# Moving the first mixture's low parts to VectorE, with two weight factors in flight and another queue order

## The chip, the cores and the metric

The kernel runs on one core of a Trainium2 chip. The metric is the device time of one launch in microseconds (us). Before the change it is 1488.94 us, the median of three runs (1488.45 to 1491.52). The core has five instruction queues that run side by side: TensorE (PE, with its weight loads as PEld), VectorE (DVE), ScalarE (ACT), GpSimd (POOL) and SyncE (SP), which here only issues DMAs. Each queue runs its own instructions in the order in which they stand in it, and waits on semaphores for the others.

## The reference, cut to what matters

Three layers follow one another: clustered attention, a feed-forward layer ("first mixture"), and a gated mixture of eight experts ("second mixture"). The change lies in the first mixture, which is

```python
h = x @ w_in                      # (1536, 512) @ (512, 2048)
g = h * (1.0 / (1.0 + np.exp(-h)))
return (g @ w_out).astype(np.float32)   # (1536, 2048) @ (2048, 512)
```

## The kernel before

All matrix products are made in fp32 accuracy from faster fp32r multiplications: each factor is rounded to a high part (a copy on ScalarE into an fp32r tile), the low part is the difference `lo = x - hi`, and a product is the sum of high x high, high x low and low x high. So each factor costs one rounding copy and one subtraction.

The first mixture is worked in four slices of 512 of the 2048 inner columns (`s` = 0 to 3). A slice has 19 steps (`u`). In steps 0 to 6 `h` is made by seven block products of a Strassen-Winograd scheme (`aproduct`, 24 matmuls each, numbers 1, 5, 6, 3, 7, 2, 4 in this order). In steps 7 to 18 twelve output tiles `y0` to `y11` are made (`ytile`, 12 or 16 matmuls each) and added into the accumulator (`total`, on ScalarE in slice 0, on VectorE after it). Product 4 of the seven (fourth counted from 0, number 7) adds into PSUM banks that product 6 uses again, so product 6 must wait for VectorE's additions `aevac`, which read these banks.

Around the products stand these pieces, named by the lines of the kernel before:

- `w_steps` (lines 82 to 100) *narrows* a quarter (128 x 512 values) of a float64 weight, read as two 32-bit words, to fp32: `wb` and `w0` on ScalarE (L88, L89), `w1` to `w4` on VectorE (L90 to L93), `wp0`, the product with the scale, on GpSimd (L94), `wp1`, an addition on VectorE (L95). A slice of `w_out` (odd `n`) is also split at once into `woh` (`wh`, ScalarE, L98) and `wol` (`wp2`, GpSimd, L99).
- `mfactor` (L120 to L125) makes the weight factor of a block product: `vh` on ScalarE (L123), `vl` on GpSimd (L124). Three pairs of buffers rotate.
- `gsilu`, `ghi`, `glo` (L665 to L679) take a finished block of `h` through silu, rounding (`gh`) and subtraction (`gl`, on GpSimd, L679).
- `split` and `five` (L127, L383) make the token-side factors from `xa`, `xb`, `xc`, which attention leaves behind; `xlo` (L367) writes them.
- `put(s, u, ...)` (L741 to L791) says at which step of which slice each of these pieces is issued; within a step the order is that of the `put` lines, after the additions and totals of the step. That order is the order in each queue. In attention a table of words (`ORDER`) does the same.

After the four slices the second mixture begins. Its first factors (`factor`, `x_factor`, `w_sums1`, L871 to L946) are written to the queues by a scheduler among the last twelve output tiles; their tiles lie in memory that the first mixture leaves.

Of the kernel before, what the change touches and what calls it, by code (L numbers as in the profile page):

```python
# [38 lines left out]
def attention_moe_kernel(ctx, tc, kq, vp, cent, w_in, w_out, w_gate, w1, w2, out):  # L39
# [687 lines left out]
    def narrow(n, k, keys):  # L727
        if (n, k) not in quarters:
            if n % 2:
                a = rp.tile([P, 1, FB], F32, name=f"a{n}_{k}", tag="na", bufs=1)  # L730
# [4 lines left out]
        for key in keys.split():
            quarters[n, k][key]()
            if key == "wp0":
                m = 4 * (n - 1) + k + 2
                load(1 + m // 4, m % 4)

    for s in range(NS1):  # L741
        n = 2 * s + 1
# [10 lines left out]
        put(s, 1, narrow, n, 1, "w1 w2")
        put(s, 2, mfactor, s, 4)
        put(s, 2, narrow, n, 0, "wp1 wh wp2")
        put(s, 2, narrow, n, 1, "w3 w4 wp0")
        put(s, 2, narrow, n, 2, "wb w0")
        put(s, 2, narrow, n, 2, "w1")
        if s == 0:
            put(s, 1, split, 7, xb)  # L760
            put(s, 2, split, 4, xa)
        put(s, 3, mfactor, s, 5)
        put(s, 3, narrow, n, 1, "wp1 wh wp2")
        put(s, 3, narrow, n, 2, "w2 w3 w4 wp0")
        put(s, 4, mfactor, s, 6)
# [560 lines left out]
```

## Time and profile before

| quantity | value |
|---|---|
| median of three runs | 1488.94 us |
| profiled execution | 1492.27 us |
| span inside it, first to last instruction | 1490.3 us |
| PE busy in the span | 1449.8 us (97%) |
| DVE, ACT, POOL busy | 1086.8, 948.6, 483.6 us |
| first mixture: first product to last output tile | 240.4 to 521.9 us |
| granted TensorE clock, mean over the span | 0.99 |

A row of a timeline gives the start, the duration, the engine, the line of the kernel, the operation with its tiles, and in brackets how long the engine had been idle before it and what ended that. A tile is named without its numbers there: `vl`, `gl` and `wol` are the low parts, `vh`, `gh` and `woh` the high parts, `y` an output tile, `b` and `raw` the pieces of the narrowing. In a row of a table by windows the first number is the length of the window, then each engine's busy time, and after the engines the granted TensorE clock as a share of full speed.

### The profile page before, as it was taken

Reading aid. Unit: us, or ns where it says so; the run is one execution under the profiler, and the core shown is the slowest. Engines: PE = TensorE matmul, PEld = TensorE weight load, DVE = VectorE, ACT = ScalarE, POOL = GpSimd, SP = SyncE. Lnnn points to the kernel's source line nnn. Section 1 sums busy time; section 2 is a strip of 40 time slices with the busy share of each in tenths; the row PEclk is TensorE's granted clock in tenths of the full one; section 3 lists DMA queues with packets and bytes.
Section 4 is the critical chain, followed back from the end, with each engine's and each line's share of the span. In section 5 each row is a group of like instructions: output and inputs, shape, how many; then the busy total and the mean of one; then the engine's idle time right before and its main releaser. Section 6 shows DMA issues by size and latency. Waiting matters only on the chain.

```text
span 1490.3 us, 25085 instructions
## 1 busy us (share of the span) xinstructions
PE 1449.8 (97%) x9785; PEld 1296.6 (87%) x9785; DVE 1086.8 (73%) x1658; ACT 948.6 (64%) x1782; POOL 483.6 (32%) x432
## 2 busy tenths in 40 slices
PE   8999998898989899999999999999999999999998
PEld 5777776787878779999999999999999999999998
DVE  7788877757777498958668577686685776866858
ACT  6677665655445257567576576675765766757655
POOL 6677744747565301020222221211211201112111
PEclk9999999899999999999999999999999999999999
DMA  7665511121212005393797987956958759569586
GB/s 205 188 167 152 139 49 45 56 71 57 71 58 100 0 29 134 74 203 81 168 159 132 189 133 141 195 86 120 159 92 160 125 96 191 90 116 166 89 149 128
DMA packets 136311, 177.48 MB, mean 119 GB/s; under 512 B 6272, under 2 KB 108672, under 8 KB 136192
## 3 DMA queue, kind: packets, MB, share of 16 engines
q0 software_dynamic: 83584, 87.30, 38.7%
q1 hardware_dynamic: 51104, 87.32, 19.4%
q8 instruction: 77, 1.26, 0.3%
q10 hardware_dynamic: 1504, 1.25, 0.3%
q14 instruction: 42, 0.34, 0.1%
HBM read 65.36 MB, written 88.87 MB: 103 GB/s over the span
## 4 chain that ended last, share of the span: by engine, by line
PE 83%; DVE 9%; ACT 3%; issue 2%; POOL 2%; DMA 0%; DVEq 0%; ACTq 0%; POOLq 0%
PE b L637 31%; PE a L637 29%; PE y L691 9%; PE av L341 4%; PE t L319 3%; PE s L282 2%; PE s L284 2%; PE l L637 2%; DVE a L92 1%; DVE h L663 1%; DVE m L291 1%; POOL wol L99 1%; DVE h L844 1%; POOL gl L679 1%; DVE b L95 1%
## 5 line engine op out<-in xcount | busy, mean ns | idle before, releaser
L637 PE MATMUL b<-wfh,ah 128*128 128x256 f32 x1344 | 381.3, 284 | 1.2 <-ACT ah L1059 1.2
L637 PE MATMUL b<-wfh,al 128*128 128x256 f32 x1344 | 381.0, 283 | 0.7 <-DVE al L1069 0.7
L637 PE MATMUL b<-wfl,ah 128*128 128x256 f32 x1344 | 380.8, 283 | 0.0
L1131 POOL DMA_DIRECT2D out_dram<-acc x87 | 126.3, 1607 | 572.5 <-ACT acc L1122 388.0
L637 PE MATMUL a<-xfh,wfh 128*128 128x512 f32 (+1 forms) x896 | 302.5, 338 | 0.0
L637 PE MATMUL a<-xfl,wfh 128*128 128x512 f32 (+1 forms) x896 | 302.0, 337 | 0.0
L637 PE MATMUL a<-xfh,wfl 128*128 128x512 f32 (+1 forms) x896 | 301.3, 336 | 0.0
L637 PEld LDWEIGHTS b<-wfh,ah 128*128 128x128 f32 x1344 | 258.1, 192 | 1.5 <-ACT ah L1059 1.4
L637 PEld LDWEIGHTS b<-wfh,al 128*128 128x128 f32 x1344 | 258.1, 192 | 1.1 <-DVE al L1069 1.1
L637 PEld LDWEIGHTS b<-wfl,ah 128*128 128x128 f32 x1344 | 258.1, 192 | 0.0
L1122 ACT ACTIVATE acc<-b,Pg 128x256 f32<-128x256 f32 x484 | 186.3, 475 | 21.8 <-issue 20.4
L847 DVE TENSOR_TENSOR al<-h,ah 128x768 fp32r<-128x768 f32 x192 | 177.7, 955 | 30.0 <-ACT ah L1061 29.4
L1061 ACT CAST ah<-h 128x768 fp32r<-128x768 f32 x192 | 160.6, 841 | 50.1 <-PE b L637 24.0
L637 PEld LDWEIGHTS a<-xfh,wfh 128*128 128x128 f32 x896 | 170.1, 190 | 19.6 <-issue 0.6
L637 PEld LDWEIGHTS a<-xfh,wfl 128*128 128x128 f32 x896 | 169.9, 190 | 18.0
L637 PEld LDWEIGHTS a<-xfl,wfh 128*128 128x128 f32 x896 | 170.1, 190 | 17.5
L847 DVE TENSOR_TENSOR wfl<-w0r,wfh 128x512 fp32r<-128x512 f32 x96 | 66.5, 708 | 81.1 <-ACT wfh L932 78.9
L844 DVE TENSOR_TENSOR h<-a,h 128x512 f32<-128x512 f32 x144 | 94.3, 686 | 26.5 <-PE a L637 25.7
L300 ACT ACTIVATE p<-s,m 128x768 f32<-128x768 f32 x96 | 86.6, 903 | 42.1 <-DVE m L291 39.4
L1048 ACT COPY h<-a 128x512 f32<-128x512 f32 x144 | 81.1, 590 | 48.2 <-PE a L637 48.1
L310 POOL TENSOR_SCALAR p<-p,rec 128x768 f32<-128x768 f32 x96 | 85.6, 904 | 55.0 <-DVE rec L305 45.0
L291 DVE TENSOR_REDUCE m<-s 128x1 f32<-128x768 f32 x96 | 89.9, 951 | 17.0 <-PE s L284 16.6
(221 smaller groups left out, 2690.8 us busy)
## 6 DMA issues: line engine op xcount, KB each, us to landing
out_dram<-acc POOLq DMA_DIRECT2D x91, 768.0 KB, 9.5
w0r<-in_w_dram SPq DMA_DIRECT2D x16, 1024.0 KB, 7.5
w1r<-in_w_dram SPq DMA_DIRECT2D x16, 1024.0 KB, 6.7
qk<-qk SPq DMA_DIRECT2D x45, 192.0 KB, 3.6
raw<-in_w_out_dram SPq DMA_DIRECT2D x16, 512.0 KB, 3.4
first_out<-acc POOLq DMA_DIRECT2D x10, 768.0 KB, 10.1
raw<-in_kq_dram SPq DMA_DIRECT2D x16, 384.0 KB, 4.2
raw<-in_w_in_dram SPq DMA_DIRECT2D x12, 512.0 KB, 3.7
```

The lines of the kernel that those rows point to most:

```text
L291: nc.vector.tensor_reduce(out=m, in_=tiles[i]["s"][:, :S], axis=AX.X, op=ALU.max, negate=True)
L300: nc.scalar.activation(t["p"], t.pop("s")[:, :S], AF.Exp, bias=t.pop("m"), accum_out=chunks[c]["sum"][:, j, 0:1])
L310: nc.gpsimd.tensor_scalar(out=p, in0=p, scalar1=chunks[c]["rec"][:, j : j + 1], scalar2=1.0, op0=ALU.mult, op1=ALU.mult)
L341: nc.tensor.matmul(ps[o * D : (o + 1) * D, :CW], lhsT=vr[2 * pair + o][:, kt, :], rhs=pts[o][:, kt, :], start=kt == 0, stop=kt == NT - 1, ...
L637: nc.tensor.matmul(ps[u][:, cols], lhsT=lf(i, k), rhs=rt(j, k), start=fresh and u not in opened, stop=k == 1 and q == 2, skip_group_check= ...
L691: nc.tensor.matmul(out, lhsT=w[:, k, d * P : (d + 1) * P], rhs=g, start=first, stop=last, skip_group_check=True)
L844: e.tensor_tensor(out=out, in0=in0, in1=in1, op=op)
L847: e.tensor_tensor(out=lo, in0=x, in1=r(hi), op=ALU.subtract)
L1048: act.copy(bank(t, u), ps[u])
L1061: act.copy(hi, x)
L1122: act.mul(t[:, 2 * u + m], z[:, m], g)
L1131: gps.dma_start(out=to, in_=t, accum_op=ALU.add)
```

## The change

All subtractions of the first mixture (`vl`, `wol`, `gl`) go from GpSimd to VectorE; GpSimd keeps only the narrowing's products `wp0`. Two pairs of factor buffers rotate instead of three, and the factors of products 2 to 6 are issued at the head of steps 1 to 5, ahead of that step's copies out of PSUM. Two `a` and three `b` buffers of the narrowing stand instead of one and two. The `put` lines are rearranged: the quarters of `w_out` are narrowed earlier, the first quarter of a later slice already in steps 17 and 18 of the slice before it. The last difference of the tokens goes into a tile of its own (`xd`), the factors of product 5 are made later in attention, and the sums `sums1` too. In the second mixture the pool of the weight sums (`wsp`) lies ahead of the token factors in memory.

```diff
-            got["wp2"] = lambda: nc.gpsimd.tensor_tensor(out=lo, in0=b, in1=r(hi), op=ALU.subtract)
+            got["wp2"] = lambda: nc.vector.tensor_tensor(out=lo, in0=b, in1=r(hi), op=ALU.subtract)
...
-        hi, lo = ((wf0 if n % 3 == 0 else wfpool[0]).tile([P, 2, FB // 2], F32R, name=f"v{c}{n}", tag=f"v{c}") for c in "hl")
+        hi, lo = ((wf0 if n % 2 == 0 else wfpool[0]).tile([P, 2, FB // 2], F32R, name=f"v{c}{n}", tag=f"v{c}") for c in "hl")
         nc.scalar.copy(hi, x)
-        nc.gpsimd.tensor_tensor(out=lo, in0=x, in1=r(hi), op=ALU.subtract)
+        nc.vector.tensor_tensor(out=lo, in0=x, in1=r(hi), op=ALU.subtract)
...
-            v(out=xa[at], in0=ps, in1=xc[at], op=ALU.subtract)
+            v(out=xd[at], in0=ps, in1=xc[at], op=ALU.subtract)
...
-    wfpool[0] = pool(mctx, "wfq", bufs=2)
+    wfpool[0] = pool(mctx, "wfq", bufs=1)
...
-            nc.gpsimd.tensor_tensor(out=t[:, m], in0=hblk[f, h][:, m], in1=r(gh)[:, h, 2 * f + m], op=ALU.subtract)
+            nc.vector.tensor_tensor(out=t[:, m], in0=hblk[f, h][:, m], in1=r(gh)[:, h, 2 * f + m], op=ALU.subtract)
...
         if s == 0:
             put(s, 0, mfactor, 0, 1)
+            put(s, 0, narrow, n, 0, "wb w0")
             put(s, 0, split, 6, xc)
-        put(s, 0, mfactor, s, 2)
+            put(s, 0, narrow, n, 0, "w1 w2 w3 w4 wp0")
+        put(s, 0, narrow, n, 0, "wp1 wh wp2")
         put(s, 0, sum4)
...
+        put(s, 0, narrow, n, 1, "wb w0 w1 w2 w3 w4 wp0")
         put(s, 1, sum3)
...
+        put(s, 4, narrow, n, 3, "wp1 wh wp2")
+        put(s, 4, ghi, 3)
+        if s == 0:
+            put(s, 4, split, 4, xd)
...
+            put(s, 17, narrow, n, 0, "wb w0 w1 w2")
+            put(s, 18, narrow, n, 0, "w3 w4 wp0")
...
+                if 1 <= u <= 5:
+                    mfactor(s, u + 1)
                 if 1 <= u <= 7:
                     aevac(s, u - 1)
...
     w2p = pool(ctx, "w2p", bufs=1)
+    wsp = pool(ctx, "wsp", bufs=2)
     xfp = pool(ctx, "xfp", bufs=1)
     wfp = pool(ctx, "wfp", bufs=5)
-    wsp = pool(ctx, "wsp", bufs=2)
```

VectorE's queue at the start of the first slice, before the change (`yl6`, `yl7` are token factors, `raw1_k`, `a1_k`, `b1_k` belong to quarter k of the first `w_out` slice):

```order
L381 TENSOR_TENSOR xa_81<-av23_3104,xc_83 128x256
L90 TENSOR_SCALAR raw1_0_3159<-raw1_0_3159 128x512
L91 TENSOR_SCALAR raw1_0_3159<-raw1_0_3159 128x512
L132 TENSOR_TENSOR yl6_3151<-xc_83,yh6_3150 128x768 x2
L115 TENSOR_TENSOR win_84<-win_84,wsum_85 128x2x256
L92 SCALAR_TENSOR_TENSOR a1_0_3165<-raw1_0_3159 128x512
L93 TENSOR_SCALAR raw1_0_3159<-a1_0_3165 128x512
```

The same queue from the same instruction after the change:

```order
L381 TENSOR_TENSOR xd_84<-av23_3105,xc_83 128x256
L124 TENSOR_TENSOR vl1_3167<-win_85,vh1_3166 128x512
L132 TENSOR_TENSOR yl6_3152<-xc_83,yh6_3151 128x768 x2
L90 TENSOR_SCALAR raw1_0_3160<-raw1_0_3160 128x512
L91 TENSOR_SCALAR raw1_0_3160<-raw1_0_3160 128x512
...
L95 TENSOR_TENSOR b1_0_3171<-a1_0_3170,b1_0_3171 128x512
L99 TENSOR_TENSOR wol_3159<-b1_0_3171,woh_3158 128x512
L115 TENSOR_TENSOR win_85<-win_85,wsum_86 128x2x256
L90 TENSOR_SCALAR raw1_1_3162<-raw1_1_3162 128x512
...
L124 TENSOR_TENSOR vl2_3228<-wsum_86,vh2_3227 128x512
```

The low part `vl2`, which product 2 needs, was on GpSimd before; it now stands behind the whole narrowing of quarter 0 and four steps of quarter 1.

ScalarE's queue in the last steps of the products of slice 1, after the change (line numbers of the changed kernel; L674 is silu, L679 the rounding of its result):

```order
L123 CAST vh12_3912<-win_85 128x512
L674 ACTIVATE h1_6_3877<-h1_6_3877 128x768 x2
L98 CAST woh_3158<-a3_3_3842 128x512
L679 CAST gh_3157<-h1_6_3877 128x768 x2
L123 CAST vh13_3950<-win_85 128x512
```

Before the change `vh13` stood right behind `vh12` and one `woh`, ahead of the silu. VectorE's queue there, after the change (L669 is an addition out of PSUM):

```order
L124 TENSOR_TENSOR vl12_3913<-win_85,vh12_3912 128x512
L669 TENSOR_TENSOR h1_6_3877<-l1_5_1_3803,h1_6_3877 128x512
...
L95 TENSOR_TENSOR b3_3_3843<-a3_3_3842,b3_3_3843 128x512
L99 TENSOR_TENSOR wol_3159<-b3_3_3843,woh_3158 128x512
L124 TENSOR_TENSOR vl13_3951<-win_85,vh13_3950 128x512
L669 TENSOR_TENSOR h1_5_3833<-l1_1_0_3757,h1_5_3833 128x512
...
L685 TENSOR_TENSOR gl1_3_3957<-h1_6_3877,gh_3157 128x768 x2
...
L685 TENSOR_TENSOR gl1_7_3994<-h1_5_3833,gh_3157 128x768 x2
```

The additions for product 6's banks (`h1_5`) stand behind `vl13`. Last, VectorE's queue at the end of the first mixture, before (`y3_7` to `y3_11` are left out, `wfl`, `xfl`, `w0r` and `ws` belong to the second mixture):

```order
L714 TENSOR_TENSOR acc1_3477<-y3_0_5121,acc1_3477 128x512
L847 TENSOR_TENSOR wfl0_5363<-w0r0_5358,wfh0_5362 128x512
L847 TENSOR_TENSOR wfl1_5367<-w0r0_5358,wfh1_5366 128x512
...
L847 TENSOR_TENSOR xfl1_5371<-acc1_3477,xfh1_5370 128x768
L714 TENSOR_TENSOR acc1_3477<-y3_5_5195,acc1_3477 128x2x256
L847 TENSOR_TENSOR xfl1_5371<-acc1_3477,xfh1_5370 128x768
L844 TENSOR_TENSOR w0r0_5358<-w0r0_5358 128x2x256
...
L714 TENSOR_TENSOR acc1_3477<-y3_11_5291,acc1_3477 128x512
L844 TENSOR_TENSOR ws0_5376<-w0r0_5358 128x512
```

and after, in the changed kernel's line numbers (L720 is the total, L851 and L848 are L847 and L844 of before):

```order
L720 TENSOR_TENSOR acc1_3480<-y3_11_5292,acc1_3480 128x512
L851 TENSOR_TENSOR wfl0_5364<-w0r0_5359,wfh0_5363 128x512
L851 TENSOR_TENSOR wfl1_5368<-w0r0_5359,wfh1_5367 128x512
L851 TENSOR_TENSOR xfl1_5372<-acc1_3480,xfh1_5371 128x768 x2
L848 TENSOR_TENSOR w0r0_5359<-w0r0_5359 128x2x256
L848 TENSOR_TENSOR ws0_5377<-w0r0_5359 128x512
```

Five subtractions and sums that stood among the last totals now stand behind the last one. The order of TensorE's and SyncE's queues is the same in both kernels.

## Rows read from the trace of the kernel before

**Rows 1.** Waits of PE in 230 to 525 us: total us, times, longest us

```profile
PE y L691 <- POOL wol L99: 10.8, 4, 2.7
PE y L691 <- POOL gl L679: 6.0, 4, 2.4
PE l L637 <- ACT h L659: 3.7, 1, 3.7
```

**Rows 2.** Busy time by windows: products and output tiles of the slices

```profile
240.40:269.80 29.40, 25.66 (x139) 22.22 (x139) 25.85 (x30) 21.19 (x35) 16.94 (x11) 0.94 0.21 65
269.80:283.20 13.40, 8.33 (x42) 6.49 (x41) 10.28 (x10) 10.66 (x17) 12.15 (x8) 0.95 0.17 55
...
316.80:346.00 29.20, 29.20 (x169) 25.84 (x168) 24.56 (x28) 20.67 (x34) 19.76 (x14) 1.00 0.17 55
346.00:352.50 6.50, 2.53 (x11) 1.45 (x9) 3.53 (x4) 5.50 (x9) 6.50 (x5) 0.83 0.27 81
352.50:385.60 33.10, 33.10 (x151) 27.80 (x152) 22.79 (x33) 9.04 (x15) 16.48 (x11) 0.93 0.21 64
...
421.20:453.80 32.60, 32.59 (x151) 27.38 (x152) 22.92 (x33) 9.07 (x15) 16.54 (x11) 0.95 0.21 65
...
489.50:522.00 32.50, 32.50 (x151) 27.28 (x152) 13.04 (x16) 5.33 (x8) 7.92 (x4) 0.95 0.00 1
```

**Rows 3.** PE's timeline: end of the gap before slice 1's output tiles

```profile
352.48 0.79 PE L691 MATMUL y<-gh,wol 128*128 128x512 f32 x1 [2.71 <-POOL wol L99]
```

**Rows 4.** VectorE's timeline, steps of the narrowing and additions, slices 0 and 1

```profile
299.33 0.43 DVE L91 TENSOR_SCALAR raw<-raw 128x512 uint32<-128x512 uint32 x1
299.80 0.69 DVE L92 SCALAR_TENSOR_TENSOR win<-raw 128x512 uint32<-128x512 uint32 x1
...
302.43 0.69 DVE L95 TENSOR_TENSOR win<-win,b 128x512 f32<-128x512 f32 x1 [1.48 <-POOL b L94]
...
319.48 1.78 DVE L115 TENSOR_TENSOR win<-win,wsum 128x512 f32<-128x512 f32 x1
...
336.11 1.87 DVE L663 TENSOR_TENSOR h<-l,h 128x512 f32<-128x512 f32 x3
```

**Rows 5.** The page's group of VectorE's 128x768 subtractions in the second mixture

```profile
L847 DVE TENSOR_TENSOR al<-h,ah 128x768 fp32r<-128x768 f32 x192 | 177.7, 955 | 30.0 <-ACT ah L1061 29.4
```

**Rows 6.** GpSimd's timeline: two low parts and a product of the narrowing

```profile
232.84 1.27 POOL L124 TENSOR_TENSOR vl<-win,vh 128x512 fp32r<-128x512 f32 x1 [1.46 <-PE av L341]
...
319.23 1.49 POOL L124 TENSOR_TENSOR vl<-wsum,vh 128x512 fp32r<-128x512 f32 x1 [2.67 <-ACT vh L123]
...
336.32 1.32 POOL L94 TENSOR_TENSOR b<-b,raw 128x512 f32<-128x512 f32 x1 [0.42 <-PE l L637]
```

**Rows 7.** ScalarE's timeline: narrowing, token factor, weight factor, silu, rounding

```profile
240.81 0.67 ACT L88 ACTIVATE b<-raw 128x512 f32<-128x512 uint32 x1
...
242.64 1.57 ACT L130 CAST yh<-xc 128x768 fp32r<-128x768 f32 x2
...
332.16 0.62 ACT L123 CAST vh<-win 128x512 fp32r<-128x512 f32 x1
...
337.42 1.58 ACT L668 ACTIVATE h<-h 128x768 f32<-128x768 f32 x2
...
339.41 1.57 ACT L673 CAST gh<-h 128x768 fp32r<-128x768 f32 x2
```

**Rows 8.** VectorE's timeline around the last total

```profile
508.08 0.69 DVE L844 TENSOR_TENSOR w0r<-w0r 128x512 f32<-128x512 f32 x1
...
522.11 0.69 DVE L714 TENSOR_TENSOR acc<-y,acc 128x512 f32<-128x512 f32 x1 [2.03 <-PE y L691]
```

**Rows 9.** PE's timeline, start of the second mixture and end of attention

```profile
529.20 1.71 PE L971 MATMUL gl<-acc,wgr 128*32 128x384 f32 x12 [2.21 <-DVE acc L844]
...
235.05 1.86 PE L319 MATMUL t<-ident,p 128*128 128x128 f32 x12 [0.79 <-POOL p L310]
```

**Rows 10.** Busy time by windows around that start

```profile
528.00:532.00 4.00, 2.79 (x22) 1.47 (x22) 3.97 (x6) 1.67 (x2) 0.00 (x0) 1.00 0.00 0
532.00:536.00 4.00, 4.00 (x21) 3.29 (x20) 3.44 (x4) 3.19 (x6) 0.00 (x0) 1.00 0.00 0
```

More of the change, by code (lines that the diff above doesn't have):

```diff
@@ L59, in attention_moe_kernel @@
     yf = {p: x_tiles(p, xpool) for p in (1, 3, 2)}
-    xa, xb, xc = (xap.tile([P, 2, S], F32, name=f"x{c}") for c in "abc")
+    xa, xb, xc, xd = (xap.tile([P, 2, S], F32, name=f"x{c}") for c in "abcd")
     NS1 = F1 // FB
@@ L380, in xlo, with five @@
         else:
-            v(out=xa[at], in0=ps, in1=xc[at], op=ALU.subtract)
-    def five(k):
+            v(out=xd[at], in0=ps, in1=xc[at], op=ALU.subtract)
+    def five():
         if 5 not in yf:
@@ L386, in five, with five_hi, five_lo @@
             yf[5] = (both[:, 0], both[:, 1])
-        split(5, xa, (k,))
+        return yf[5]
+    def five_hi(k):
+        nc.scalar.copy(five()[0][:, k], xa[:, k])
+    def five_lo(k):
+        nc.vector.tensor_tensor(out=five()[1][:, k], in0=xa[:, k], in1=r(five()[0][:, k]), op=ALU.subtract)
     def wd(k):
@@ L412, in attention_moe_kernel @@
         KINDS[key] = (wstep(key), 1, 0, 4)
-    KINDS["y5a"] = (lambda i: five(0), 1, 6, 7)
-    KINDS["y5b"] = (lambda i: five(1), 1, 6, 7)
+    KINDS["h5"] = (five_hi, 1, 0, 2)
+    KINDS["l5"] = (five_lo, 1, 0, 2)
     KINDS["s1"] = early(sums1)
@@ L421, in attention_moe_kernel @@
         wp0,-2 T,-1 evD,-3 S,3 evD,-1 lv,2 evA,-2 wp1,-2 sim,1,0 rec,0 lv,1 av,-1 mx,2 ld,5 nrm,0 mx,3 ex,2 nrm,1 ex,3 split,3 S,4 xh,-1 rec,1
-        wb,-1 w0,-1 xl,-1 y5a,0 T,0 sims,1 mx,4 T,1 evA,0 nrm,2 S,5 sd,3 evD,1 ex,4 simt,1,1 nrm,3 T,2 mx,5 cc,2 T,3 evA,2 split,2 T,4 cha,1 ex,5 T,5 chb,1 S,6
-        evD,4 evA,3 S,7 chc,1 evA,5 mx,6 av,0 chd,1 ex,6 mx,7 chs,1 rec,2 ex,7 sd,2 nrm,4 S,8 chr,1 rec,3 xh,0 nrm,5 oht,1,0 mx,8 T,6 mr,1 S,9
-        nrm,6 xl,0 y5b,0 s1,0 ex,8 md,1 T,7 evD,6 nrm,7 T,8 mx,9 evA,7 T,9 castm,4 evA,8 T,10 evD,9 ex,9 T,11 castm,5 evD,10 ld,6 S,10 evA,11 wd,0 w1,-1 S,11
+        wb,-1 w0,-1 xl,-1 T,0 sims,1 mx,4 T,1 evA,0 nrm,2 S,5 sd,3 evD,1 ex,4 simt,1,1 nrm,3 T,2 mx,5 cc,2 T,3 evA,2 split,2 T,4 cha,1 ex,5 T,5 chb,1 S,6
+        evD,4 evA,3 S,7 chc,1 evA,5 h5,-6 mx,6 av,0 chd,1 ex,6 mx,7 chs,1 rec,2 ex,7 sd,2 nrm,4 S,8 l5,-6 chr,1 rec,3 xh,0 nrm,5 oht,1,0 mx,8 T,6 mr,1 S,9
+        nrm,6 xl,0 ex,8 md,1 T,7 evD,6 nrm,7 T,8 mx,9 evA,7 T,9 castm,4 s1,0 evA,8 T,10 evD,9 ex,9 T,11 castm,5 evD,10 ld,6 S,10 evA,11 wd,0 w1,-1 S,11
         rec,4 w2,-1 av,1 mx,10 castd,5 nrm,8 mx,11 ex,10 nrm,9 ex,11 f0,0
@@ L729, in narrow @@
             if n % 2:
-                a = rp.tile([P, 1, FB], F32, name=f"a{n}_{k}", tag="na", bufs=1)
-                b = rp.tile([P, 1, FB], F32, name=f"b{n}_{k}", tag="nb")
+                a = rp.tile([P, 1, FB], F32, name=f"a{n}_{k}", tag="na")
+                b = rp.tile([P, 1, FB], F32, name=f"b{n}_{k}", tag="nb", bufs=3)
                 quarters[n, k] = w_steps(n, k, a, b, wo_h[:, k : k + 1], wo_l[:, k : k + 1])
             else:
-                quarters[n, k] = w_steps(n, k, win[:, :, k * P : (k + 1) * P], rp.tile([P, 4, P], F32, name=f"b{n}_{k}", tag="nb"))
+                quarters[n, k] = w_steps(n, k, win[:, :, k * P : (k + 1) * P], rp.tile([P, 4, P], F32, name=f"b{n}_{k}", tag="nb", bufs=3))
         for key in keys.split():
@@ L742, in attention_moe_kernel @@
         n = 2 * s + 1
-        put(s, 0, narrow, n, 0, "wb w0 w1 w2")
         if s == 0:
             put(s, 0, mfactor, 0, 1)
+            put(s, 0, narrow, n, 0, "wb w0")
             put(s, 0, split, 6, xc)
-        put(s, 0, mfactor, s, 2)
+            put(s, 0, narrow, n, 0, "w1 w2 w3 w4 wp0")
+        put(s, 0, narrow, n, 0, "wp1 wh wp2")
         put(s, 0, sum4)
-        put(s, 1, mfactor, s, 3)
-        put(s, 1, narrow, n, 0, "w3 w4 wp0")
-        put(s, 1, narrow, n, 1, "wb w0")
+        put(s, 0, narrow, n, 1, "wb w0 w1 w2 w3 w4 wp0")
@@ L752, in attention_moe_kernel @@
         put(s, 1, sum3)
[L753 to L758, printed above, removed]
-        if s == 0:
[L760 to L765, printed above, removed]
@@ L766, in attention_moe_kernel @@
-        put(s, 4, narrow, n, 3, "wb w0")
+        put(s, 1, narrow, n, 1, "wp1 wh wp2")
+        put(s, 1, narrow, n, 2, "wb w0 w1 w2")
+        if s == 0:
+            put(s, 2, split, 7, xb)
+        put(s, 2, narrow, n, 2, "w3 w4 wp0")
+        put(s, 2, narrow, n, 3, "wb w0")
+        put(s, 2, narrow, n, 2, "wp1 wh wp2")
+        put(s, 3, narrow, n, 3, "w1 w2 w3 w4 wp0")
         put(s, 4, gsilu, 3)
-        put(s, 4, narrow, n, 2, "wp1 wh wp2")
-        put(s, 4, narrow, n, 3, "w1")
-        put(s, 5, ghi, 3)
+        put(s, 4, narrow, n, 3, "wp1 wh wp2")
@@ L771, in attention_moe_kernel @@
+        put(s, 4, ghi, 3)
+        if s == 0:
+            put(s, 4, split, 4, xd)
         put(s, 5, glo, s, 3)
         put(s, 5, gsilu, 7)
-        put(s, 5, narrow, n, 3, "w2 w3 w4 wp0")
-        put(s, 6, ghi, 7)
+        put(s, 5, ghi, 7)
         put(s, 6, glo, s, 7)
         put(s, 6, gsilu, 2)
-        put(s, 6, narrow, n, 3, "wp1 wh wp2")
-        put(s, 7, ghi, 2)
+        put(s, 6, ghi, 2)
         put(s, 7, glo, s, 2)
-        put(s, 7, ghi, 4)
-        put(s, 7, glo, s, 4)
+        last = int(s < NS1 - 1)
@@ L782, in attention_moe_kernel @@
+        put(s, 7 + last, ghi, 4)
+        put(s, 7 + last, glo, s, 4)
         if s < NS1 - 1:
             n += 1
-            for k, u in enumerate((7, 9, 12, 14)):
-                put(s, u - 1 if k else u, narrow, n, k, "wb w0")
-                put(s, u, narrow, n, k, "w1 w2")
+            for k in range(4):
+                u = 8 + 2 * k
+                put(s, u, narrow, n, k, "wb w0 w1 w2")
                 put(s, u + 1, narrow, n, k, "w3 w4 wp0")
@@ L789, in attention_moe_kernel @@
             put(s, 15, mfactor, s + 1, 0)
-            put(s, 17, sums1)
-            put(s, 18, mfactor, s + 1, 1)
+            put(s, 16, sums1)
+            put(s, 17, mfactor, s + 1, 1)
+            n += 1
+            put(s, 17, narrow, n, 0, "wb w0 w1 w2")
+            put(s, 18, narrow, n, 0, "w3 w4 wp0")
     load(1, 0)
```

## The prediction

> **What bounds the kernel now.** I read the page first (TensorE busy 97%, so a gain can only come out of its gaps or its clock), then its waits, then the windows of the first mixture, then the timelines of the queues that release it. In the waits [rows 1] the reader is to see that three releasers hold TensorE up between 230 and 525 us: `wol` 10.8 us in four waits, `gl` 6.0 in four, and one 3.7 us wait for a high part `gh` in slice 0. That is 20.5 us. All but the 3.7 are GpSimd's, and they stand at the start of the output tiles of each slice: 2.71 for `wol` ahead of slice 1's [rows 3], and in the window around it TensorE is busy 2.53 of 6.50 us [rows 2], so 3.97 of gap. Slices 2 and 3 repeat this. Slice 0 loses 2.71 + 2.4 + 3.73 = 8.8.
>
> The windows show a second cost: after each such gap the granted clock falls to 0.93 to 0.95 for the whole block of output tiles, while the products of slice 1, without a gap, ran at 1.00 [rows 2]. The three blocks of slices 1 to 3 lose 0.07 x 33.1 + 0.05 x 32.6 + 0.05 x 32.5 = 5.6 us by it. (Such a mean lies between the two levels, 2.4 and 1.2 GHz: some part of the block ran at the lower one.) A gap alone doesn't do it: after the 2.21 us wait at 529.2 [rows 9] the clock stayed at 1.00 [rows 10].
>
> Without gaps a slice would be 29.2 us of products (4.17 each) and about 33 of output tiles, some 62.3.
>
> **Unit prices.** On VectorE a step of the narrowing takes 0.43 or 0.69 [rows 4], so the four steps `w1` to `w4` of a quarter 2.1 with issue between; a 512-column subtraction 0.64 (955 ns for 768 columns [rows 5], times 2/3), about 0.65 start to start, up to 0.69 [rows 4]; a `gl` pair 1.85; three additions out of PSUM 1.87 [rows 4]. On ScalarE a factor is 0.62, a silu pair 1.58, a rounding pair 1.57, a first pair of narrowing steps 1.35 [rows 7]. GpSimd's product is 1.32, a subtraction there 1.27 to 1.49 [rows 6].
>
> VectorE and GpSimd disturb one another: a sum at 319.48 took 1.78 us instead of 0.69, beside GpSimd's subtraction of 319.23, itself 1.49 instead of 1.27; but three additions that read PSUM took 1.87 right beside a GpSimd product of 336.32 [rows 4, 6]. The Trainium skill ("SBUF — State Buffer", section "SBUF: two separate sides") calls the port pair that the two share an exclusive lock, held for a whole instruction by whichever starts first, and names two SBUF inputs as a case that needs it. The rows agree: the two-input sum is held up, the additions out of PSUM are not. By that rule each product left on GpSimd may cost VectorE its full 1.32; I count less in the sum, since in the narrowing VectorE waits for that product anyhow (1.48 idle ahead of `wp1` [rows 4]).
>
> **Term A, slices 1 to 3.** GpSimd loses per slice 7 `vl`, 4 `wol`, 4 `gl` pairs and keeps 8 products, 10.6 us. All `wol` are ready in step 4, long before the output tiles. Their two waits go. What is late next is the factor of product 6. Take the slice's start as 0. With two buffers `vh12` must wait until product 3 ends, at 4 x 4.17 = 16.7. Then `vh12` 0.62, `vl12` 0.68, a hold by the product up to 0.62, three additions 1.87; silu can start at 20.5, ends at 22.1, `woh` 0.5, `gh` 1.5, and only then `vh13` 0.55, `vl13` 0.68, and the first addition for product 6's bank 0.61: 25.9. TensorE is free at 6 x 4.17 = 25.0. The gap is 0.9 (0.3 where the product doesn't collide, 2.5 where it collides twice). Of the last `gl` pair that the first output tiles need (`gl1_7`) the first half comes at about 31.7, wanted at 31.9: no gap, with little to spare. So 3.97 becomes 0.9, **3 x 3.07 = -9.2** (-4.4 to -11).
>
> **Clock.** If gaps of 0.9 leave the clock as the 2.21 one did, nearly all of the 5.6 comes back: **-5.0** (0 to -6.5; slice 0's share is in term B).
>
> **Term B, slice 0.** Here nothing of the slice was narrowed ahead, and all that the put lines moved ahead stands in front of `vl2`. From 240.43 as 0: VectorE ends attention's tail at 1.27, `vl1` 1.95, the `yl6` pair 5.0 (ScalarE's `yh6` ends at 4.0), four steps 7.1, GpSimd's product 8.5, `wp1`, `wol`, `sum4` 10.45, four steps of quarter 1 12.55, `vl2` 13.2. Product 2 wants it at 8.8 (its first matmuls need only `vh`). Gap 4.4; product 2 ends at 16.9 and product 3, after 0.3 for `vl3`, at 21.3. Then `yl7`, two steps, a product's wait and three subtractions bring `vl4` at 23.9, wanted 21.8: gap 2.1; product 5 ends at 31.75. Quarter 3's steps end at 26.0, `vl5` 26.65, additions 28.5, silu 30.1, `woh` 30.65, `gh` 32.15, `yh4` 33.7, `yl4` 34.65, `vl6` 35.3, first addition 35.95: gap 4.2. Together 11.0 in place of 8.8, +2.2; and the clock, which lost 0.06 x 25.7 and 0.05 x 8.3 in the product windows [rows 2], may lose 0.8 more. **+3.0**. If the queues overlap better than I chain them, the gap at product 2 alone remains, -4; if holds add a product each, +6.
>
> **Term C, into the second mixture.** Two `wfl`, an `xfl` pair and a weight step, 0.68 + 0.62 + 1.82 + 0.69 = 3.8 us, which ran among the last totals, now stand behind the last total, 522.11 [rows 8]. TensorE needs the first of these at once: total, two `wfl` and half the `xfl` pair make 0.69 + 0.68 + 0.62 + 0.91 = 2.9 of wait. The wait at 529.2 [rows 9] is for VectorE's `ws` step, which stands behind all of them, so it ends later by the whole run, 3.8, less about 0.1 of issue: **+3.7** (0 if TensorE's first matmuls, on high parts, cover the run, +5.5 if the old 2.21 grows too).
>
> **Term D, end of attention.** `vl0` leaves GpSimd, whose `p` TensorE waits 0.79 for [rows 9]; the sums and the `yf5` subtractions change places. **-0.5** (-2.5 to +1).
>
> **The sum.** -9.2 - 5.0 + 3.0 + 3.7 - 0.5 = -8.0. The profiled execution's 1492.27 would be 1484.3; it stands 3.3 above the median of 1488.94, so the median becomes **1481**.
>
> **Rivals.** R1, VectorE becomes the bound (slower). Its load in a slice: eight quarters at 3 x 0.43 + 0.69 + 0.69 = 2.67 make 21.4, the moved subtractions 7.2 + 7.6, nine additions 5.6, twelve totals 8.3, four sums 2.6: 52.7 of 62.3 us. If every product on GpSimd holds it for the whole 1.32, eight make 10.6 and it is 63.3: no idle left, and each late piece is late for TensorE. Then slices 1 to 3 gain nothing in gaps or clock and +3.0 + 3.7 - 0.5 remains: 1498 profiled, **1495**. It decides when the holds pass some 9.6 us a slice. For it speaks the 1.78; against it that additions and totals read PSUM, and that VectorE idles during a product already. Chance 0.09.
>
> R2, the clock stays low in the output tiles, as it did after gaps of 3.97: -3.0, **1486**. For it: the clock was at 0.95 in slice 0's products too, so one gap early might be enough. Chance 0.16.
>
> R3, slice 0 and the way into the second mixture are cheap, since both chains count every instruction in a row: B -4, C +1.5, so -17.2: **1472**. Chance 0.20.
>
> R4, both are dear and the clock comes back by 2 only: -9.2 - 2 + 6 + 5.5 - 0.5 = -0.2: **1488.7**. Chance 0.09.
>
> The forecast has 0.46, with its own range of 1476 to 1486.
>
> **How the numbers follow.** Under 0.2% (3 us) this kernel can't be told from no change. Faster than 1486: the forecast 0.44, R3 0.20, R2 0.10, R4 0.01, together 0.75. Slower than 1492: R1 0.07, R4 0.03, so 0.10. Between: 0.15. The range of 1470 to 1490 leaves out R1, half of R4 and the far half of R3.
>
> **What would show it.** Right: no wait for `wol` or `gl` from GpSimd in slices 1 to 3; a gap under 1 us ahead of product 6, released by VectorE; output tiles at 1.00; in slice 0 gaps of about 4.4, 2.1 and 4.2 ahead of products 2, 4 and 6; about 3 us on the low part right after the last output tile. Wrong: two-input steps of VectorE at 1.8 us all through the slices with TensorE waiting for `vl` (R1); gaps gone but output tiles still at 0.93 to 0.95 (R2); the products of slice 0 without the 4 us gaps, or the second mixture starting without one (R3).

## The result and the profile after

| | before | after |
|---|---|---|
| median | 1490.03 us (4 runs, 1488.45 to 1491.52) | 1473.72 us (4 runs, 1473.14 to 1474.04) |
| profiled execution, its span | 1492.27, 1490.3 | 1473.80, 1472.0 |

The ratio is 0.989, with a 95% interval of 0.9873 to 0.9907: 16.3 us faster, where 8 were forecast. Between the two profiled executions it is 18.5.

The waits of TensorE between 230 and 525 us in the changed kernel, as in [rows 1] (total us, times, longest):

```profile
PE l L643 <- DVE h L669: 4.6, 4, 3.1
PE l L643 <- DVE vl L124: 3.1, 1, 3.1
PE a L643 <- DVE xfl L851: 2.6, 1, 2.6
PE t L319 <- POOL p L310: 1.8, 1, 1.8
PE gl L975 <- DVE acc L848: 1.2, 1, 1.2
PE l L643 <- ACT h L665: 0.7, 1, 0.7
```

No wait for `wol` or `gl` is left. The windows of slice 0 (products, output tiles) and slice 1 (the same), columns as in [rows 2]:

```profile
235.50:276.60 41.10, 34.26 (x169) 28.53 (x169) 33.24 (x53) 28.88 (x46) 5.91 (x4) 0.88 0.17 52
276.60:309.60 33.00, 33.00 (x163) 27.90 (x162) 19.39 (x33) 17.74 (x30) 5.64 (x5) 1.00 0.21 64
309.60:339.80 30.20, 29.47 (x170) 25.77 (x169) 24.41 (x38) 20.05 (x34) 5.31 (x4) 1.00 0.24 71
339.80:372.70 32.90, 32.90 (x162) 27.84 (x161) 27.07 (x46) 14.42 (x23) 5.87 (x5) 1.00 0.21 65
```

The output tiles run without a gap at a granted clock of 1.00; slice 0's products, at 0.88 and with 6.8 us of gaps, grew most, from 34.93 to 41.15 us. Smaller losses are gaps of 0.73, 0.40 and 0.41 us ahead of product 6 in slices 1 to 3, and a new wait at the start of the second mixture. TensorE's timeline shows the gaps of slice 0, that of slice 1 and that of the second mixture:

```profile
244.81 0.50 PE L643 MATMUL l<-yh,vh 128*128 128x512 f32 x1 [0.70 <-ACT h L665]
...
248.62 0.79 PE L643 MATMUL l<-yh,vl 128*128 128x512 f32 x1 [3.08 <-DVE vl L124]
...
270.78 0.65 PE L643 MATMUL l<-yh,vh 128*128 128x512 f32 x1 [3.06 <-DVE h L669]
...
335.51 0.47 PE L643 MATMUL l<-yh,vh 128*128 128x512 f32 x1 [0.73 <-DVE h L669]
...
501.35 0.50 PE L643 MATMUL a<-xfl,wfh 128*128 128x512 f32 x1 [2.62 <-DVE xfl L851]
```

By stages, each the difference of two starts in TensorE's timeline (the first matmul of a slice, or the first after the last piece of the gate, the `gl<-acc,wgr` matmuls of the second mixture). Each column is one profiled execution. The last four columns are experiments of the next section:

| stage, us | before | after | e1 | e2 | e8 | e12 |
|---|---|---|---|---|---|---|
| start to first product | 240.43 | 235.48 | 240.19 | 235.74 | 239.65 | 237.56 |
| slice 0 | 76.18 | 74.11 | 70.36 | 74.10 | 71.30 | 69.00 |
| slice 1 | 68.80 | 63.15 | 64.83 | 63.13 | 62.13 | 62.1 |
| slice 2 | 68.24 | 62.78 | 64.89 | 62.84 | 62.13 | 62.1 |
| slice 3 | 68.26 | 62.82 | 63.28 | 62.82 | 62.14 | 62.13 |
| into the second mixture | 18.89 | 22.55 | 20.14 | 20.39 | 22.55 | 20.31 |
| rest of the span | 949.5 | 951.1 | 948.1 | 947.8 | 949.6 | 948.0 |

From before to after: -4.95, -2.07, -16.55 for three slices, +3.66, +1.6: together -18.3.

### The profile page after: what moved, and what is told of

Read it like the earlier page. It is cut to its first block, busy times and chain, and to the rows that moved or that the text cites. A ratio compares the mean times of both kernels' runs of the same rounds, so it can differ in the third digit from the quotient of the medians.

```text
span 1472.0 us, 25066 instructions
## 1 busy us (share of the span) xinstructions
PE 1443.1 (98%) x9784; PEld 1293.4 (88%) x9785; DVE 1092.0 (74%) x1734; ACT 948.6 (64%) x1782; POOL 361.3 (25%) x356
## 4 chain that ended last, share of the span: by engine, by line
PE 77%; DVE 3%; ACT 2%; issue 0%; DVEq 0%; ACTq 0%
PE b L643 33%; PE a L643 30%; PE y L697 9%; PE l L643 5%; DVE vl L124 1%; DVE h L848 1%; DVE h L669 1%; ACT h L674 0%; ACT gh L679 0%; DVE wfl L851 0%; DVE xfl L851 0%; ACT vh L123 0%; PE gl L975 0%; DVE h L1154 0%; ACT woh L98 0%
## 5 line engine op out<-in xcount | busy, mean ns | idle before, releaser
L851 DVE TENSOR_TENSOR al<-h,ah 128x768 fp32r<-128x768 f32 x192 | 177.7, 954 | 30.2 <-ACT ah L1065 29.6
L851 DVE TENSOR_TENSOR wfl<-w0r,wfh 128x512 fp32r<-128x512 f32 x96 | 64.8, 690 | 81.1 <-ACT wfh L936 79.0
L848 DVE TENSOR_TENSOR h<-a,h 128x512 f32<-128x512 f32 x144 | 94.2, 685 | 26.4 <-PE a L643 25.6
## 6 DMA issues: line engine op xcount, KB each, us to landing
first_out<-acc POOLq DMA_DIRECT2D x10, 768.0 KB, 10.6
```

Source lines behind the costliest of these rows:

```text
L848: e.tensor_tensor(out=out, in0=in0, in1=in1, op=op)
L851: e.tensor_tensor(out=lo, in0=x, in1=r(hi), op=ALU.subtract)
```

## Experiments

Theory: the engine of the three subtractions carries the gain, and the new order and memory places add in some stages and cost in others. Rival: the order carries it. Differences of 1 to 2 us between medians are near the noise: where the 95% intervals of two ratios overlap, the text says so.

**e1, the engine alone.** From the kernel before:

```diff
-            got["wp2"] = lambda: nc.gpsimd.tensor_tensor(out=lo, in0=b, in1=r(hi), op=ALU.subtract)
+            got["wp2"] = lambda: nc.vector.tensor_tensor(out=lo, in0=b, in1=r(hi), op=ALU.subtract)
...
-        nc.gpsimd.tensor_tensor(out=lo, in0=x, in1=r(hi), op=ALU.subtract)
+        nc.vector.tensor_tensor(out=lo, in0=x, in1=r(hi), op=ALU.subtract)
...
-            nc.gpsimd.tensor_tensor(out=t[:, m], in0=hblk[f, h][:, m], in1=r(gh)[:, h, 2 * f + m], op=ALU.subtract)
+            nc.vector.tensor_tensor(out=t[:, m], in0=hblk[f, h][:, m], in1=r(gh)[:, h, 2 * f + m], op=ALU.subtract)
```

> The kernel before with only the engine of the three subtractions (vl, wol, gl) changed to VectorE; order, three factor buffers, attention and memory places as before. Theory: the engine is what counts. A gl pair takes 1.85 us on VectorE in place of some 3.5 on GpSimd, a wol 0.65 in place of 1.3 to 1.7, so the last gl and wol come before TensorE needs them: the waits of 3.97 us at the start of each block of output tiles in slices 1 to 3 and of 5.1 in slice 0 shrink under 1 us, the clock in the tiles comes back (5.6 us), the 3.73 wait of slice 0 stays, nothing moves behind the last total: about 1490 - 12 - 5 - 4 = 1469 us. Rival: the order counts. In the old order VectorE is full with narrowing in steps 5 and 6, wol of quarter 3 still comes last, gaps of 2 us a slice and the low clock stay: 1482 us or more.

Measured: 1472.55 us (1470.95 to 1474.22), ratio 0.9878 (0.9863 to 0.9894): near the theory's 1469, and no different from the whole change. Its waits on the output tiles:

```profile
PE y L691 <- DVE wol L99: 3.3, 3, 1.1
PE y L691 <- DVE gl L679: 2.6, 4, 0.8
...
PE y L691 <- ACT woh L98: 0.5, 3, 0.2
```

Beside [rows 1] the waits on the output tiles are 6.4 us in place of 16.8. The table shows what the rest of the change then does: slices 1 to 3 are 4.25 us shorter with the new order (188.75 against 193.00), slice 0 is 3.75 longer, the way into the second mixture 2.4 longer, attention 4.7 shorter in these two executions.

**e11, gl alone.** From the kernel before, only the last of those three lines:

```diff
-            nc.gpsimd.tensor_tensor(out=t[:, m], in0=hblk[f, h][:, m], in1=r(gh)[:, h, 2 * f + m], op=ALU.subtract)
+            nc.vector.tensor_tensor(out=t[:, m], in0=hblk[f, h][:, m], in1=r(gh)[:, h, 2 * f + m], op=ALU.subtract)
```

> The kernel before with gl alone on VectorE; vl and wol stay on GpSimd, order, buffers and places as before. Theory: wol was late because it stood behind gl in GpSimd's queue, so with gl gone both waits shrink: gaps of about 1 us in place of 3.97 in slices 1 to 3, clock mostly back, slice 0 3 us better: 1474 to 1476, most of what the whole change gives. Rival: wol is late by its own place (the last steps of the products) and by GpSimd's 1.3 to 1.7 us: its 2.7 waits and the low clock stay and only the gl waits go: 1484 to 1486.

Measured: 1477.76 us, ratio 0.9919 (0.9906 to 0.9931): 12.1 of the 16.3 us, somewhat less than the theory. GpSimd's queue in slice 1, of the kernel before and then of e11:

```profile
340.90 3.85 POOL L679 TENSOR_TENSOR gl<-h,gh 128x768 fp32r<-128x768 f32 x2
345.90 1.30 POOL L94 TENSOR_TENSOR b<-b,raw 128x512 f32<-128x512 f32 x1 [1.15 <-issue]
347.16 4.04 POOL L679 TENSOR_TENSOR gl<-h,gh 128x768 fp32r<-128x768 f32 x2
351.16 1.26 POOL L99 TENSOR_TENSOR wol<-b,woh 128x512 fp32r<-128x512 f32 x1
```

```profile
341.55 1.31 POOL L94 TENSOR_TENSOR b<-b,raw 128x512 f32<-128x512 f32 x1 [4.04 <-issue]
345.69 1.27 POOL L99 TENSOR_TENSOR wol<-b,woh 128x512 fp32r<-128x512 f32 x1 [2.83 <-DVE b L95]
```

The last `wol` stood behind a `gl` pair of 4.04 us. With `gl` gone it starts when its input is there, and TensorE waits 1.7 for it in place of 2.71.

**e5, e6, e7: one subtraction back on GpSimd.** From the changed kernel, one of the three lines reversed each (`vector` to `gpsimd` for `gl`, for `wol`, for `vl`).

```diff
-            nc.vector.tensor_tensor(out=t[:, m], in0=hblk[f, h][:, m], in1=r(gh)[:, h, 2 * f + m], op=ALU.subtract)
+            nc.gpsimd.tensor_tensor(out=t[:, m], in0=hblk[f, h][:, m], in1=r(gh)[:, h, 2 * f + m], op=ALU.subtract)
```

> The changed kernel with gl alone back on GpSimd. Theory: with wol early and GpSimd empty, a gl pair of some 3.3 us there still comes nearly in time; gl7 is 0 to 0.6 us late a slice, the clock stays: 1473.7 to 1475.5. Rival: gl's engine was half of the gain; the 1.2 us wait for gl comes back in each slice, and the low clock of the output tiles with it: 1480 us or more.

> The changed kernel with wol alone back on GpSimd. Theory: wol is now made in steps 0 to 4, some 9 us before it is used, so its engine no longer matters: 1473.7 within 1, no wait for wol. Rival: GpSimd's wol of 1.3 to 1.7 us hold VectorE's two-input steps by turns, the chain through silu and product 6's bank gets longer by about 1 us a slice: 1477 or more.

> The changed kernel with vl alone back on GpSimd. Theory: vl was never late in the kernel before, and on VectorE it stands behind the narrowing; back on GpSimd vl2 of slice 0 comes some 2.8 us earlier (0.5 wait in place of 3.08, clock behind it better), the additions for product 6's bank no longer wait behind vl: 1470. Rival: vl on GpSimd takes 1.3 to 1.5 us instead of 0.68 and holds VectorE, so that product 6 waits for vl by 0.5 to 1 us more in every slice: 1475 to 1477.

Measured: `gl` 1479.37 (ratio 0.9925, 0.9910 to 0.9939), `wol` 1473.96, `vl` 1472.01. So `gl` is worth 5.7 us in the new order and `wol` nothing that can be told from noise. `vl` back on GpSimd is 1.7 faster by the medians, but the intervals (0.9863 to 0.9896, and 0.9873 to 0.9907 for the change) overlap, so all that is shown is that `vl` on VectorE gains nothing. For `gl` the size was near the rival's, but neither mechanism holds: in slices 1 to 3 TensorE waits only 0.2 for `gl` in a slice, and the clock stays at 1.00. GpSimd holds VectorE up. In slice 0 of e5, GpSimd and then VectorE:

```profile
268.21 4.33 POOL L685 TENSOR_TENSOR gl<-h,gh 128x768 fp32r<-128x768 f32 x2 [2.96 <-ACT gh L679]
```

```profile
269.63 3.71 DVE L132 TENSOR_TENSOR yl<-xd,yh 128x768 fp32r<-128x768 f32 x2 [1.51 <-ACT yh L130]
```

The `yl` pair takes 3.71 us where it takes 1.83 in the changed kernel; the additions behind it are late, and product 6 waits 4.84 in place of 3.06. The low clock behind that wait lasts longer too. Its window in e5:

```profile
273.60:280.50 6.90, 5.80 (x15) 4.67 (x16) 3.94 (x7) 4.72 (x7) 2.34 (x2) 0.51 0.01 2
```

In slices 1 to 3 product 6 waits about 0.9 in place of 0.4 to 0.7, for the same reason (the `vl` ahead of the additions took 1.19 us in place of 0.69 in slice 1). This is the case of two SBUF inputs that the Trainium skill names ("SBUF — State Buffer", "SBUF: two separate sides").

For `vl` the time went the way of the theory, but not by its reason: `vl2` was later still, since on GpSimd it stood behind the product of quarter 1 (a wait of 5.43 in place of 3.08). Product 6 waited 0.92 in place of 3.06, so the two waits together are no shorter. Yet slice 0 is 1.45 us shorter in the profile. What differs in its favour is the clock, which fell at product 6's wait in the changed kernel and stayed up here:

```profile
272.00:276.00 4.00, 3.79 (x20) 3.23 (x21) 4.00 (x7) 2.70 (x4) 0.60 (x1) 1.00 0.02 4
```

One combination was not run: the new order with all three subtractions on GpSimd. If the three single steps add, the engine is worth some 4 us in the new order (5.7 + 0.2 - 1.7), which would leave some 12 to the order, while e1 shows the engine alone giving all of it in the old order. Either alone may thus do most of the work, and how the two share the gain of the changed kernel stays open.

**e8, the narrowing's products on VectorE too** (attention's narrowing among them).

```diff
-            wp0=lambda: nc.gpsimd.tensor_tensor(out=b, in0=b, in1=u, op=ALU.mult),
+            wp0=lambda: nc.vector.tensor_tensor(out=b, in0=b, in1=u, op=ALU.mult),
```

> The changed kernel with the narrowing's product on VectorE too, GpSimd left empty: a measure of what the products on GpSimd cost VectorE. Theory: a product costs 0.69 on VectorE in place of a hand-over of 1.5 us and of vl held from 0.68 to 1.82 beside it; vl2 of slice 0 comes about 1 us earlier and the 0.73 gap of slice 1 falls to 0.4; VectorE has 58 of 62 us to do a slice and keeps up: 1472. Rival: VectorE is full, late pieces stand in its queue, gaps ahead of product 6 or at the output tiles grow by 1 us a slice: 1477.

Measured: 1472.34 us (ratio 0.9878, 0.9864 to 0.9893), the theory's number, though this interval overlaps the changed kernel's. The profile prices what GpSimd still costs VectorE. In slice 1 of the changed kernel, GpSimd's product and then VectorE's low part beside it; last the same low part in e8:

```profile
326.87 1.30 POOL L94 TENSOR_TENSOR b<-b,raw 128x512 f32<-128x512 f32 x1 [4.25 <-ACT vh L123]
```

```profile
326.90 1.82 DVE L124 TENSOR_TENSOR vl<-win,vh 128x512 fp32r<-128x512 f32 x1 [0.16 <-ACT vh L123]
```

```profile
328.26 0.69 DVE L124 TENSOR_TENSOR vl<-win,vh 128x512 fp32r<-128x512 f32 x1 [0.67 <-ACT vh L123]
```

In e8 slices 1 to 3 have no gap at all (62.13 us each), so the products on GpSimd cost 0.65 to 1.0 a slice, holds and hand-over together; VectorE does its 54.8 us of slice 1 in time. Slice 0 is 2.8 shorter. In this execution 4.2 us are given back ahead of the first product: VectorE has attention's products there as well, and the clock was at 0.83 from 230 to 240 us. Which of the two did it is not shown.

**e4, attention's old words.** The changed kernel with the table `ORDER` of before, and for its words:

```diff
-    KINDS["h5"] = (five_hi, 1, 0, 2)
-    KINDS["l5"] = (five_lo, 1, 0, 2)
+    KINDS["y5a"] = (lambda i: (five_hi(0), five_lo(0)), 1, 6, 7)
+    KINDS["y5b"] = (lambda i: (five_hi(1), five_lo(1)), 1, 6, 7)
```

> The changed kernel with the old table of words in attention (the two token-factor pieces of product 5 and the sums at their old places). Theory: the new order in attention is worth the waits for pt and p that TensorE had between 185 and 230 us (0.83 + 0.30 + 1.24 + 0.68 + 0.58 us less the 0.38 and the larger 1.84 wait of the changed kernel), about 2.5 us: 1476.2, with the 1.24 wait near 200 us back. Rival: attention differs between the two traces by the clock in the first 30 us alone, which is not of the order, and the old words cost nothing: 1473.7 within 0.7.

Measured: 1475.76 us (ratio 0.99, 0.9886 to 0.9915), 2.0 over the changed kernel: near the theory, but the intervals overlap, so the time alone doesn't decide. TensorE's timeline does, where the waits come back:

```profile
187.56 0.66 PE L319 MATMUL t<-ident,p 128*128 128x128 f32 x4 [0.83 <-DVE pt L327]
188.52 0.66 PE L319 MATMUL t<-ident,p 128*128 128x128 f32 x4 [0.30 <-ACT pt L327]
197.84 1.50 PE L319 MATMUL t<-ident,p 128*128 128x128 f32 x12 [1.24 <-ACT pt L327]
```

and VectorE and ScalarE show what stood in the way, a piece of the token factor of product 5 ahead of `pt`, the copies of transposed blocks out of PSUM that TensorE's gaps here wait for:

```profile
196.37 0.96 DVE L393 TENSOR_TENSOR yf<-xa,yf 128x768 fp32r<-128x768 f32 x1 [0.48 <-ACT yf L390]
```

```profile
195.51 0.83 ACT L390 CAST yf<-xa 128x768 fp32r<-128x768 f32 x1
```

The first product starts at 238.43 there, at 235.48 in the changed kernel.

**e2, the sums' memory back in its old place.**

```diff
-    wsp = pool(ctx, "wsp", bufs=2)
     xfp = pool(ctx, "xfp", bufs=1)
     wfp = pool(ctx, "wfp", bufs=5)
+    wsp = pool(ctx, "wsp", bufs=2)
```

> The changed kernel with the pool of the weight sums (wsp) back behind the token factors; five VectorE instructions then stand among the last totals again instead of behind the last. Theory: this place costs what the traces show, 3.66 us from the last output tile to the product after the gate, and the clock at 500 to 510 and at 540 to 545 us another 1.6: 1473.7 - 3.7 = 1470.0, or 1468.4 with the later clock. The 2.62 wait for xfl goes, the 1.22 wait for acc becomes 2.2. Rival: TensorE waits there for something else and the place is worth nothing: 1473 to 1474.

Measured: 1468.92 us (1468.45 to 1470.63), ratio 0.9856 (0.9841 to 0.9871): 4.8 less than the changed kernel, the theory with the later clock. In the changed kernel these stand behind the last total, to be read beside [rows 8]:

```profile
498.54 0.69 DVE L720 TENSOR_TENSOR acc<-y,acc 128x512 f32<-128x512 f32 x1 [2.03 <-PE y L697]
499.15 1.28 DVE L851 TENSOR_TENSOR wfl<-w0r,wfh 128x512 fp32r<-128x512 f32 x2
500.35 1.82 DVE L851 TENSOR_TENSOR xfl<-acc,xfh 128x768 fp32r<-128x768 f32 x2
502.08 0.68 DVE L848 TENSOR_TENSOR w0r<-w0r 128x512 f32<-128x512 f32 x1
```

VectorE had idled 2.03 to 2.10 us ahead of each of the last nine totals, so there was room; with the old place they run earlier, and `ws` follows the last total of e2 at once:

```profile
498.83 0.69 DVE L720 TENSOR_TENSOR acc<-y,acc 128x512 f32<-128x512 f32 x1 [2.03 <-PE y L697]
499.44 0.68 DVE L848 TENSOR_TENSOR ws<-w0r 128x512 f32<-128x512 f32 x1
```

In the table the last two rows have to be read together, since in e2 the clock was low once on the way (a mean of 0.76 from 505 to 512 us): they are 968.2 us in e2 and 968.4 before, against 973.7 in the changed kernel.

**e3, vl2 earlier.** From the changed kernel:

```diff
             put(s, 0, split, 6, xc)
+            put(s, 0, mfactor, 0, 2)
             put(s, 0, narrow, n, 0, "w1 w2 w3 w4 wp0")
...
-                if 1 <= u <= 5:
+                if 1 <= u <= 5 and (s or u > 1):
```

> The changed kernel with the factor of product 2 of slice 0 issued in step 0 right behind the yl6 pair, ahead of quarter 0's narrowing steps. Theory: the 3.08 wait for vl2 is due to its place in VectorE's queue alone; it goes, with the low clock behind it (some 2 us from 249 to 253): 1473.7 - 5 = 1468.6. Rival: the work of slice 0 is a chain through narrowing, silu and product 6's bank, and what is gained at product 2 is given back at product 6, whose wait of 3.06 grows to 5 or 6: 1472 to 1474.

Measured: 1473.22 us, the rival's time, but not its reason. The 3.08 wait for `vl2` is gone; product 6 still waits 3.08, where the rival had 5 or 6. What was gained is lost sooner: 1.04 at the start of product 2 (0.70 in the changed kernel), 1.79 ahead of product 3 and 1.65 within it. Slice 0 is 75.71 against 74.11.

**e9 and e10, the order of slice 0.** From the changed kernel with the sums' memory back (e10 with e8's line too):

```diff
-        put(s, 0, narrow, n, 1, "wb w0 w1 w2 w3 w4 wp0")
+        put(s, int(s == 0), narrow, n, 1, "wb w0 w1 w2 w3 w4 wp0")
...
+        if s == 0:
+            put(s, 3, split, 4, xd)
...
+        put(s, 4, mfactor, s, 6)
         put(s, 4, ghi, 3)
-        if s == 0:
-            put(s, 4, split, 4, xd)
...
-                if 1 <= u <= 5:
+                if 1 <= u <= 4:
```

> The changed kernel with the sums' pool back behind the token factors and three moves: in slice 0 quarter 1's narrowing one step later (so vl2 stands right behind sum4) and the token factor yh4, yl4 two steps ahead of silu; in all slices the factor of product 6 ahead of the first rounding gh. Theory: vl2 and the additions for product 6's bank are late only by what stands ahead of them in VectorE's and ScalarE's queues; both 3.06 waits of slice 0 fall under 0.7, those of slices 1 to 3 go, slice 0's clock returns by 2 to 4 us: 1468.9 (measured with the sums back) - 4.8 - 1.4 - 3 = 1460. Rival: slice 0 is a chain, as with vl2 moved alone; the waits turn up at products 3 to 5 or at the first output tiles: 1467 to 1469.

> The same with the narrowing's product on VectorE as well. Theory: the hand-over to GpSimd and back (1.5 us a quarter) stands in slice 0's chain and nowhere else, VectorE has the room: 1 to 2 us less than with the products on GpSimd, 1459. Rival: with slice 0 unblocked VectorE is the engine that is late, and the products there add 0.69 each to the chain: 1 us more than on GpSimd.

Measured: e9 1464.51 us (ratio 0.9832, 0.9819 to 0.9845), e10 1466.17 (0.9842, 0.9828 to 0.9855). Slices 1 to 3 came out as said, without a gap. Slice 0 did not: 71.09 us, 3.0 gained where about 8 were expected, because waits turned up at the products between. In e9:

```profile
PE l L643 <- DVE vl L124: 4.6, 3, 2.1
...
PE l L643 <- DVE h L669: 1.0, 1, 1.0
```

e10 is no better; the ranges of its runs (1464.63 to 1467.09) and e9's (1463.31 to 1465.92) overlap, so which is faster stays open.

**e12, slice 0's narrowing spread out.** From e9, in slice 0 only, for each quarter the last steps one step later (quarter 2's two), and quarter 3's in steps 4 and 5:

```diff
-        put(s, 0, narrow, n, 0, "wp1 wh wp2")
+            put(s, 1, narrow, n, 0, "wp1 wh wp2")
...
-        put(s, 1, narrow, n, 1, "wp1 wh wp2")
+            put(s, 2, narrow, n, 1, "wp1 wh wp2")
...
-        put(s, 4, narrow, n, 3, "wp1 wh wp2")
+            put(s, 5, narrow, n, 3, "wp1 wh wp2")
```

> The kernel of e9 with slice 0's narrowing spread one step later throughout (a quarter's last steps never in the step that follows its first), slices 1 to 3 as there. Theory: what is left in slice 0 of e9 (2.07, 0.87 and 1.65 for vl, 1.00 for the bank) is narrowing ahead of vl in VectorE's queue; spread out, vl2 and vl3 come in time and 2 to 4 us with their clock are saved: 1461. Rival: the first slice has all its narrowing and all its token factors to do in 36 us and only moves its waits to the first output tiles (wol of quarter 3): 1464 to 1466.

Measured: 1463.10 us (1460.85 to 1463.83), ratio 0.9813 (0.9800 to 0.9826), between the two. Slice 0 is 69.00 us, with these waits left in it:

```profile
PE l L643 <- DVE h L669: 2.2, 1, 2.2
...
PE l L643 <- DVE vl L124: 1.3, 2, 1.0
```

Its median is the lowest of all, 10.6 us under the changed kernel. Its range overlaps e9's, so by the times alone it is open whether it beats e9; in the profile slice 0 is 2.1 shorter than there.

## Why the prediction was right, and where its terms were not

The direction, the main mechanism and the stated range of 1470 to 1490 were right. The forecast's own narrower range, 1476 to 1486, was missed by 2.3 us, on the fast side. The terms add up to -8.0, and the stages of the two profiled executions to -18.3: two terms, B and D, were wrong by some 5 each and A by 2.4, all on the same side, and 1.6 was lost later. That the forecast of 1481 is only 7 too high, and not 10, comes from the 3.3 us by which the profiled execution before stood above its median and which the prediction took off; some 2 of them turn up again in term D.

**Term A and the clock** held. The waits for `wol` and `gl` went, the gap ahead of product 6 was 0.73, 0.40 and 0.41 where 0.9 was reckoned, and the clock in the output tiles returned in full: 32.96 us a block. Together -16.55 against -14.2. The output tiles of these slices became 18.9 us shorter. 11.7 of this are the waits for `wol` and `gl` ([rows 1] less slice 0's 5.1), and the rest, some 7, goes with the clock, for which 5.0 was reckoned. The 0.93 to 0.95 did not lie evenly over a block: in slice 1 of the kernel before the clock was at 0.50 up to 357.0 us and at 1.00 behind that. What was not foreseen is that the engine alone does most of it (e1), `gl` first (e11).

**Term B failed, with the wrong sign** (+3.0, measured -2.07). The step that failed is "Together 11.0 in place of 8.8, +2.2; and the clock ... may lose 0.8 more". The chain itself was near: `vl2` was reckoned to end at 13.2 and ended at 13.1, and the products of slice 0 grew from 34.93 to 41.15, 6.2 where 8.1 follow from the step (11.0 less the 3.73 of before, and 0.8). (The 2.1 gap at product 4 didn't show: `vl4` ended at 23.98, as reckoned, but TensorE, slowed by its clock, wanted it no earlier.) That the products came out near is partly luck: the gaps in them were 6.8 where 11.0 were reckoned, and the clock took some 5.1 (41.15 less 29.17 without loss and 6.84 of gaps) where 2.0 and 0.8 were. It was at the lower level behind both long waits, ahead of product 2's low part and of product 6:

```profile
250.00:253.00 3.00, 3.00 (x8) 2.31 (x7) 2.86 (x7) 2.93 (x6) 0.00 (x0) 0.50 0.59 175
271.00:274.00 3.00, 3.00 (x8) 2.33 (x8) 3.00 (x5) 2.14 (x3) 0.00 (x0) 0.50 0.02 5
```

What was left out is the clock in slice 0's output tiles. I counted that loss for slices 1 to 3 and wrote that slice 0's share was in term B, but there I looked at the products alone. The window I did not read, of the kernel before:

```profile
283.20:316.60 33.40, 33.40 (x150) 27.98 (x151) 16.95 (x22) 13.49 (x23) 15.24 (x10) 0.92 0.21 64
```

The tiles went from 41.25 to 32.96: 5.1 of gaps, which were counted, and 3.2 of clock and the like, which were not.

**Term C** held: +3.66 against +3.7, by the wait for the low parts and the `ws` step, and e2 shows that the memory place is the cause. In the profiled execution of the changed kernel 1.6 more followed at 540 to 545 us by the clock (the last rows of this text).

**Term D failed** (-0.5, measured -4.95). Two things are in it. Some 2 to 3 us are the words: e4 puts the first product 2.95 later, and the time 2.0. I read only TensorE's wait at 235 [rows 9] and not those near 190 and 200, where, as e4 shows, the pieces that the change moves stood ahead of the copies TensorE needed; the 235 wait even grew to 1.84. The other 2 us are not the change's: the kernel before was profiled at a clock of 0.66 between 10 and 20 us, the changed one at 1.00. Executions with the changed attention show the low clock too, and their first products stand at 237.59 and 237.56. A start can differ without that, too: e9's first product, with the same attention and no low clock there, stands at 236.86, so the split is good to some 1.4 us. The rows are of the kernel before, the changed kernel, e6 and e12:

```profile
10.00:20.00 10.00, 8.56 (x40) 5.69 (x40) 6.62 (x15) 5.47 (x12) 4.62 (x6) 0.66 0.85 233
```

```profile
10.00:20.00 10.00, 7.71 (x49) 5.00 (x51) 7.25 (x17) 7.14 (x16) 6.29 (x7) 1.00 0.85 235
```

```profile
10.00:20.00 10.00, 8.66 (x44) 4.96 (x42) 7.21 (x17) 5.95 (x13) 5.06 (x6) 0.83 0.81 227
```

```profile
10.00:20.00 10.00, 8.03 (x35) 5.67 (x40) 6.48 (x15) 5.39 (x12) 4.53 (x6) 0.66 0.85 233
```

**Rivals.** R1 fell: VectorE was busy 24.41 + 27.07 = 51.5 us of slice 1's 63.1, near the 52.7 reckoned (where four `gl` pairs at 1.85 make 7.4 and not 7.6), and the holds by GpSimd cost 0.65 to 1.0 us a slice (e8). R2 fell, the clock came back. R3 gave the nearest number, 1472, but for another reason: the way into the second mixture was not cheap, and slice 0's products were nearly as dear as reckoned. R4 fell with B.
